# Ring loads of a weight stream pause around the reads of turned exponentials

## The chip, the cores and the metric

The kernel runs on one core of a Trainium2 chip. The metric is the device time of one execution in microseconds (us): the median of three runs is 900.81 us (900.17 to 900.99). The core has TensorE (PE, with its weight loads shown as PEld), VectorE (DVE), ScalarE (ACT), GpSimd (POOL) and SyncE (SP); SP issues nearly all DMAs of this kernel on one queue.

## The reference

The inputs are q, k and v of 8 batches, 8 heads, 576 tokens and 64 features, and the weights of a gated feed-forward layer (512 to 1536 to 512).

```python
scores = scale * np.matmul(q_c, k_c.transpose(0, 1, 2, 4, 3))   # chunks of 64 tokens
scores = scores - np.max(scores, axis=-1, keepdims=True)
attn = np.exp(scores)
attn = attn / (np.sum(attn, axis=-1, keepdims=True) + 1e-09)
out = np.matmul(attn, v_c)
...
x = out of all heads, one row of 512 per token                  # 4608 rows
rms = np.sqrt(np.mean(x * x, axis=-1, keepdims=True) + 1e-06)
xn = x / rms * rms_g
g = xn @ w_gate
silu = g * (1.0 / (1.0 + np.exp(-g)))
val = xn @ w_val
return (silu * val @ w_out).astype(np.float32)
```

## The kernel before, in words

Tokens go through in tiles of 512. The first three tiles (`PLAIN`) are computed plainly, each float32 product as three products of rounded high and low parts. The other six are taken two at a time, in three blocks (`for b in range(NB)`, L1237), by a scheme that computes a 2x2 product of blocks with seven products (`P1` to `P7`) in place of eight. The text calls b = 0, 1 and 2 block one, two and three.

A block has two halves. The up half is six calls of `up_pair` (L832), each with seven products, so 42 steps, numbered 0 to 41 by `step.n`; a step is 12 matmuls of 128x512. The down half has 42 more. At the end of each step, `step()` runs what the table `at` holds for that number. There the attention of the next block's tokens is put, four units of 256 tokens each. Unit n starts at step `PAIR_AT[n]` (2, 12, 22, 32), and its parts come at the offsets in `PAIR_STEPS`: scores at 0, `second` at 3, `third` at 5, `fourth` at 8. `second` turns the exponentials on VectorE and writes them to DRAM (`turn`, L359, two DMAs `away_e<-e`, L367). `third` reads them back in another layout (`turn_back`, L369, eight DMAs of 64 KB, `eT<-away_e`, L376). `fourth` multiplies them by the values on TensorE (`ps_o`, L393). So the reads of units 0, 1 and 2 stand in the program at the end of steps 7, 17 and 27, and the products that need them behind steps 10, 20 and 30. Block three carries no attention.

The weights of the up half's products lie in DRAM as 21 pieces of 1 MB. `ring_load` (L809) takes one of the 18 buffers of the pool `wts` and issues one DMA (L812, `wr<-wsd`). Piece m holds products 2m and 2m + 1, which from pair 1 on are steps 2m and 2m + 1. The first three pieces are loaded before the block. In the loop, `ring_load_ahead(n // 2)` keeps three pieces ahead, so that from step 6 on an even step s stands in the program with the load of piece s/2 + 2: piece 5 at step 6, piece 6 at step 8, 10 at step 16, 11 at 18, 15 at 26, 16 at 28. The same pool holds the products' inputs (`xp`) and results (`g`, `tt`), and the down half's weights (`wo`).

What sets the order: TensorE's instructions are kept in the order of the program (`manual_schedule`, L1155). In the down half ACT, DVE and SP are too (`IN_ORDER`, L1265). In the up half the framework's scheduler orders these: by priority, which is the place in the program unless `high_priority` moves it, among the instructions that its own timing takes to be ready and that have a buffer. Once ordered, SP's queue runs in that order, and an instruction that waits holds up those behind it.

Of the kernel before, what the change touches and what calls it, by code (L numbers as in the profile page):

```python
# [42 lines left out]
PAIR_STEPS = -4, 0, 3, 5, 8, 8, 8, 11, 13  # L43
# [3 lines left out]
PAIR_AT = 2, 12, 22, 32  # L47
# [13 lines left out]
NB = (NT - PLAIN) // 2  # L61
# [19 lines left out]
def tile_chunk_attn_swiglu(  # L81
# [40 lines left out]
    last = Last()  # L122
    wp = last.open("wp", 3)

    def urgent():

        return tc.high_priority(offset=URGENT)

    def bank(pool, name):
        return pool.tile([P, 512], F32, tag=pool_tag[id(pool)], name=name)  # L130
# [614 lines left out]
    def big(shape, dtype, name):  # L745
        return wts.tile(shape, dtype, tag="wts", name=name)
# [62 lines left out]
    def ring_load(n):  # L809
        if n < len(wsd):  # L810
            t = ring[n] = big([P, 2, 2, 2, KH], F32R, "wr")
            nc.sync.dma_start(t.rearrange("p n a m c -> p n (a m c)").bitcast(F32), wsd[n])  # L812

    def product(n, m, p, ps, start, stop):
        w = ring[n // 2][:, n % 2]
        xp = xside[p]
        for kt in range(2):
            cols = slice(kt * P, (kt + 1) * P)
            for i, (a, b) in enumerate(((0, 0), (0, 1), (1, 0))):
                nc.tensor.matmul(  # L820
                    ps,
                    w[:, a, m, cols],
                    xp[:, b, kt],
                    start=start and kt == 0 and i == 0,
                    stop=stop and kt == 1 and i == 2,
                    skip_group_check=True,
                )
# [1 line left out]
    def hold(name):  # L829
        return xs.tile([P, TT], F32, tag="xs", name=name)  # L830

    def up_pair(i, step, wos, tt, sums, last=None):  # L832

        g = big([P, 2, 2, TT], F32, "g")
        ps = [{} for _ in range(2)]
        kept = [{} for _ in range(2)]

        def bank_of(m, name, pool):
            ps[m][name] = bank(pool, f"ps_{name}")

        for k, p in enumerate(ORD if i else FIRST):
            n = 7 * i + p
            ring_load_ahead(n // 2)
            if i == NPR - 1 and k in (4, 6):
                wos.append(out_load(k // 2 - 2))
            for m in range(2):
                if p == P1:
                    bank_of(m, "a", ps_h)
                elif p in (P6, P5, P4):
                    bank_of(m, {P6: "b", P5: "c", P4: "d"}[p], ps_acc)  # L850
                b = ps[m][{P1: "a", P2: "a", P6: "b", P7: "b", P5: "c", P3: "c", P4: "d"}[p]]
                product(n, m, p, b, p in (P1, P6, P5, P4), p in (P2, P7, P3, P4))
            if k == 6 and last is not None:
                with urgent():
                    last()
            with urgent():
                after(p, ps, kept, g)
            if k == 1 and sums:
                sums.pop()()
            step()  # L860
        if i % PER == 0:
            tt.append(big([P, PER, TT], F32, "tt"))
        t = tt[-1][:, i % PER]

        def sum_up():
            nc.vector.tensor_tensor(t, g[:, 0, 1], g[:, 0, 0], op=ALU.subtract)
            nc.vector.tensor_tensor(g[:, 0, 1], g[:, 1, 1], g[:, 0, 1], op=ALU.subtract)

        sums.append(sum_up)
        return g, t  # L870
# [47 lines left out]
    def ring_load_ahead(n):  # L918
        while loaded[0] < min(n + AHEAD_R, len(wsd)):
            ring_load(loaded[0])  # L920
            loaded[0] += 1
# [10 lines left out]
    def out_load(n):  # L932
        t = big([P, PER, 2, OH], F32R, "wo")
        part = t[:, : osd[n].shape[1]].rearrange("p n a c -> p n (a c)")
        nc.sync.dma_start(part.bitcast(F32), osd[n])
        return t

    def split_high(src, ready):
        gh = tmp.tile([P, TT], F32R, tag="tmp", name="gh")
        nc.scalar.copy(gh, src)  # L940
        ready.append([gh])

    def split_low(src, pair):
        gl = gp.tile([P, TT], F32R, name="gl")
        nc.vector.tensor_tensor(gl, src, pair[0].bitcast(F32), op=ALU.subtract)  # L945
        pair.append(gl)
# [102 lines left out]
    def unit_steps(u, x):  # L1049

        both = 2 * u, 2 * u + 1

        def first():
            sc = two_banks(ps_a, "ps_s")
            for i in both:
                scores(i, sc)
            turned_softmax(u, sc)

        def second():
            for i in both:  # L1060
                turned_sum(i)
                turn(i)

        def third():
            for i in both:
                turn_back(i)

        def fourth():
            turned_values(u)

        def fifth():
            for i in both:
                turned_norm(i)

        def sixth():
            for i in both:
                turned_scale(i)

        return [
            lambda: load_unit(u),  # L1080
            first,
            second,
            third,
            fourth,
            fifth,
            sixth,
            lambda: turn_x(u),
            lambda: turn_x_back(u, x),
        ]
# [147 lines left out]
    for b in range(NB):  # L1237
        t = PLAIN + 2 * b
        at = early
        early = {}  # L1240
        if b + 1 < NB:
            u = 2 * t + 4
            for n in range(4):
                for k, f in enumerate(unit_steps(u + n, (x, x2)[n // 2])):
                    after_it = LAST_STEPS if b == 0 and n == 3 else PAIR_STEPS
                    at.setdefault(max(PAIR_AT[n] + after_it[k], 0), []).append(f)
            one, two, late = x_sides(x, x2, st)
            for n, f in enumerate(one[:2]):
                at.setdefault(PAIR_AT[1] + PAIR_STEPS[-1] + 4 + n, []).append(f)
            for n, f in zip(X_AT, one[2:] + two[:1] + two[4:] + two[1:4]):  # L1250
                at.setdefault(7 * NPR + n, []).append(f)
            early = {n: list(todo) for n, todo in enumerate(late)}
        step = Steps(at)
        gts, wos, tt, sums, ready = [], [], [], [], []

        def first_splits():
            for g, _ in gts[:2]:
                split_high(g[:, 0, 0], ready)
            split_low(gts[0][0][:, 0, 0], ready[0])

        for i in range(NPR):
            last_part = first_splits if i == NPR - 1 else None
            gts.append(up_pair(i, step, wos, tt, sums, last_part))
        loaded[0] = 0
        with tc.manual_schedule(engines=IN_ORDER):  # L1265
            down_pair(t, gts, wos, step, b + 1 < NB, sums, ready)
# [53 lines left out]
```

## Time and profile before

| what | value |
|---|---|
| median of three runs | 900.81 us (900.17 to 900.99) |
| profiled execution | 901.91 us, its span 900.1 us |
| granted TensorE clock, mean | 0.990 |
| PE, DVE, ACT, POOL busy | 98%, 67%, 51%, 20% of the span |
| mean DMA rate | 258 GB/s |
| loads of ring pieces (L812) | 63 of 1024 KB, 7.0 us to landing at the median |
| reads of exponentials (L376) | 112 of 64 KB, 3.6 us to landing at the median |

The span runs from the first to the last instruction; the profiled execution's own time is 1.8 us more. A row of the timeline gives the start, the length, the engine, the line, and what is written from what; the rows of SP are the issues of DMAs, not the transfers. Block one's up half runs from 355.2 to 482.5 us, that of block two from 540.7 to 666.8.

### The profile page before, as it was taken

What the parts mean: (1) busy time and instruction counts of PE and PEld (TensorE: products, weight loads), DVE (VectorE), ACT (ScalarE), POOL (GpSimd) and SP (SyncE); (2) the same over time, 40 slices, a digit from 0 to 9 for tenths busy, and PEclk for the clock granted to TensorE, in tenths of its full rate; (3) what the DMA queues carried; (4) which work ended last, traced back from release to release, by engine and by line L of the source; (5) the groups of instructions that cost most, each with busy time, mean ns of one, the idle gap of its engine ahead of it and who ended that gap; (6) DMA issues with size and microseconds to landing.
All of it is one profiled execution on the core that took longest, in us unless ns stands there. A gap on an engine that the chain in (4) does not pass through costs nothing.

```text
span 900.1 us, 17442 instructions
## 1 busy us (share of the span) xinstructions
PE 879.5 (98%) x6828; PEld 721.1 (80%) x6828; DVE 607.0 (67%) x962; ACT 455.9 (51%) x775; POOL 181.7 (20%) x157
## 2 busy tenths in 40 slices
PE   4899999999999999999999999999999999999998
PEld 3688888888888888887887888888878888888886
DVE  6999865464568755985677997556669953334776
ACT  5997934343435564545455644336547522222452
POOL 0003040243200000233233002333330004323200
PEclk9799999999999999999999999999999999999999
DMA  9699999777977865688977887687667784445442
GB/s 355 269 342 328 324 327 359 246 244 244 305 240 242 249 210 163 263 304 276 300 264 263 298 316 278 247 301 225 242 243 277 285 354 169 155 154 201 183 164 95
DMA packets 85794, 231.84 MB, mean 258 GB/s; under 512 B 8912, under 2 KB 45264, under 8 KB 71504
## 3 DMA queue, kind: packets, MB, share of 16 engines
q1 hardware_dynamic: 84656, 230.20, 72.5%
q8 instruction: 54, 0.88, 0.4%
q10 hardware_dynamic: 1056, 0.52, 0.2%
q14 instruction: 28, 0.23, 0.1%
HBM read 167.25 MB, written 63.44 MB: 256 GB/s over the span
## 4 chain that ended last, share of the span: by engine, by line
PE 84%; ACT 6%; DVE 4%; DMA 4%; issue 1%; POOL 1%; SPq 0%; ACTq 0%; DVEq 0%; POOLq 0%
PE ps_a L820 10%; PE ps_c L820 10%; PE ps_b L820 10%; PE ps_g L592 9%; PE acc L627 9%; PE ps_v L592 9%; PE ps_c L1033 5%; PE ps_b L1033 5%; PE ps_a L1033 5%; PE ps_d L820 5%; PE ps_d L1033 3%; PE ps_o L393 2%; PE ps_s L266 2%; DMA raw<-w_up_dram 1%; ACT w L178 1%
## 5 line engine op out<-in xcount | busy, mean ns | idle before, releaser
L820 PE MATMUL ps_b<-xp,wr 128*128 128x512 f32 x432 | 104.6, 391 | 0.0
L820 PE MATMUL ps_c<-xp,wr 128*128 128x512 f32 x432 | 104.0, 390 | 0.0
L820 PE MATMUL ps_a<-xp,wr 128*128 128x512 f32 x432 | 103.8, 390 | 0.0
L592 PE MATMUL ps_g<-xh,parts 128*128 128x512 f32 x288 | 96.8, 397 | 0.6 <-ACT xh L517 0.6
L592 PE MATMUL ps_v<-xh,parts 128*128 128x512 f32 x288 | 95.2, 391 | 0.4 <-DVE sg L614 0.4
L820 PEld LDWEIGHTS ps_c<-xp,wr 128*128 128x128 f32 x432 | 80.9, 188 | 16.9
L820 PEld LDWEIGHTS ps_a<-xp,wr 128*128 128x128 f32 x432 | 80.8, 188 | 17.0
L820 PEld LDWEIGHTS ps_b<-xp,wr 128*128 128x128 f32 x432 | 80.6, 188 | 17.0
L627 PE MATMUL acc<-parts,gh 128*128 128x512 f32 x288 | 89.9, 393 | 0.0
L908 POOL TENSOR_TENSOR g<-u,u 128x512 f32<-128x512 f32 x18 | 23.2, 1289 | 252.6 <-DVE u L904 141.3
L592 PEld LDWEIGHTS ps_g<-xh,parts 128*128 128x128 f32 x288 | 54.7, 190 | 12.8 <-ACT xh L517 1.0
L592 PEld LDWEIGHTS ps_v<-xh,parts 128*128 128x128 f32 x288 | 54.4, 189 | 12.0 <-DVE sg L614 0.8
L940 ACT CAST gh<-g 128x512 fp32r<-128x512 f32 x72 | 43.5, 621 | 37.9 <-PE ps_b L1033 13.2
L627 PEld LDWEIGHTS acc<-parts,gh 128*128 128x128 f32 x288 | 53.2, 188 | 11.2
L945 DVE TENSOR_TENSOR gl<-g,gh 128x512 fp32r<-128x512 f32 x72 | 49.2, 692 | 16.2 <-PE ps_a L1033 5.7
L876 ACT ACTIVATE p<-p 128x512 f32<-128x512 f32 x36 | 22.7, 632 | 70.2 <-POOL p L898 60.0
L898 POOL TENSOR_TENSOR p<-p,p 128x512 f32<-128x512 f32 x36 | 46.9, 1313 | 53.6 <-DVE rs L354 35.7
L592 PE MATMUL ps_g<-xl,parts 128*128 128x512 f32 x144 | 56.7, 394 | 0.0
L592 PE MATMUL ps_v<-xl,parts 128*128 128x512 f32 x144 | 56.3, 391 | 0.0
L627 PE MATMUL acc<-parts,gl 128*128 128x512 f32 x144 | 56.2, 390 | 0.0
L885 DVE TENSOR_TENSOR u<-ps_b,p 128x512 f32<-128x512 f32 x36 | 24.7, 687 | 41.2 <-PE ps_b L820 37.6
L820 PE MATMUL ps_d<-xp,wr 128*128 128x512 f32 x216 | 52.3, 391 | 0.0
(150 smaller groups left out, 1706.4 us busy)
## 6 DMA issues: line engine op xcount, KB each, us to landing
wr<-wsd SPq DMA_DIRECT2D x63, 1024.0 KB, 7.0
wo<-osd SPq DMA_DIRECT2D x30, 1024.0 KB, 7.7
raw<-w_up_dram SPq DMA_DIRECT2D x12, 1024.0 KB, 10.4
vt<-v_dram SPq DMA_DIRECT2D x18, 512.0 KB, 7.0
wsd<-parts SPq DMA_DIRECT2D x18, 512.0 KB, 8.4
qt<-qT_dram SPq DMA_DIRECT2D x17, 512.0 KB, 5.8
kt<-kT_dram SPq DMA_DIRECT2D x17, 512.0 KB, 6.8
away_e<-e SPq DMA_DIRECT2D x28, 256.0 KB, 3.3
```

The lines of the kernel that those rows point to most:

```text
L266: nc.tensor.matmul(st["s"][j][c * CH : (c + 1) * CH, pr], st["q"][rows, pr, tok : tok + CH], st["k"][rows, pr, tok : tok + CH], start=True ...
L393: nc.tensor.matmul(st["o"][(2 * c + t) * Q : (2 * c + t + 1) * Q, h * D : (h + 1) * D], eT[c][rows, t, h], vt[rows, c, h], start=True, sto ...
L592: nc.tensor.matmul(ps, a[f][:, cols], b[dt], start=(dt == 0 and i == 0), stop=(dt == NDT - 1 and i == 2),)
L627: nc.tensor.matmul(acc[s], a[:, cols], b, start=(f == 0 and i == 0), stop=(f == NF - 1 and i == 2),)
L820: nc.tensor.matmul(ps, w[:, a, m, cols], xp[:, b, kt], start=start and kt == 0 and i == 0, stop=stop and kt == 1 and i == 2, skip_group_ch ...
L876: nc.scalar.activation(t, t if src is None else src, AF.Silu)
L885: nc.vector.tensor_tensor(kp["u2"], b["b"], kp["p1"], op=add)
L898: nc.gpsimd.tensor_tensor(kp["p5"], kp["p1"], kp["p5"], op=add)
L908: nc.gpsimd.tensor_tensor(g[:, 0, 1], kp["u2"], kept[0]["u2"], op=mult)
L940: nc.scalar.copy(gh, src)
L945: nc.vector.tensor_tensor(gl, src, pair[0].bitcast(F32), op=ALU.subtract)
L1033: nc.tensor.matmul(banks[m][name], w[:, (0, 1, 0)[k], m * P : (m + 1) * P], (gh, gh, gl)[k], start=opens and i == 0 and k == 0, stop=not ( ...
```

## The change

In blocks one and two, `up_pair` does not call `ring_load_ahead` in the steps 6, 7, 16, 17, 26 and 27. The next call, in steps 8, 18 and 28, loads what was left out together with its own piece: 5 and 6, 10 and 11, 15 and 16. Odd steps load nothing from step 5 on in either version. No instruction is added or removed.

```diff
-    def up_pair(i, step, wos, tt, sums, last=None):
+    def up_pair(i, step, pauses, wos, tt, sums, last=None):
...
             n = 7 * i + p
-            ring_load_ahead(n // 2)
+            if step.n not in pauses:
+                ring_load_ahead(n // 2)
...
         step = Steps(at)
+        reads = [n + PAIR_STEPS[3] for n in PAIR_AT[:-1]] if b + 1 < NB else []
+        pauses = {n - k for n in reads for k in range(2)}
...
-            gts.append(up_pair(i, step, wos, tt, sums, last_part))
+            gts.append(up_pair(i, step, pauses, wos, tt, sums, last_part))
```

## Rows read from the trace of the kernel before

**Rows 1.** The page: span, and busy time of each engine.

```profile
span 900.1 us, 17442 instructions
...
PE 879.5 (98%) x6828; PEld 721.1 (80%) x6828; DVE 607.0 (67%) x962; ACT 455.9 (51%) x775; POOL 181.7 (20%) x157
```

**Rows 2.** Waits of PE, 355 to 482.6: us in total, times, longest.

```profile
PE ps_o L393 <- DMA eT<-away_e: 0.7, 2, 0.4
```

**Rows 3.** Timeline of PE, block one: start, length, what.

```profile
386.49 1.48 PE L393 MATMUL ps_o<-vt,eT 64*32 64x64 f32 x128
...
413.84 2.88 PE L820 MATMUL ps_d<-xp,wr 128*128 128x512 f32 x12
416.73 0.27 PE L393 MATMUL ps_o<-vt,eT 64*32 64x64 f32 x2
...
418.09 1.42 PE L393 MATMUL ps_o<-vt,eT 64*32 64x64 f32 x122 [0.26 <-DMA eT<-away_e]
```

**Rows 4.** The chain that ended last, 400 to 425: start, length, what.

```profile
408.14 8.06 DMA wr<-wsd
...
416.22 1.74 DMA eT<-away_e
```

**Rows 5.** Timeline of SP, block one.

```profile
357.23 2.03 SPq L812 DMA_DIRECT2D wr<-wsd  x4
...
378.93 3.68 SPq L376 DMA_DIRECT2D eT<-away_e  x8
...
383.60 0.44 SPq L812 DMA_DIRECT2D wr<-wsd  x1
...
398.80 1.10 SPq L812 DMA_DIRECT2D wr<-wsd  x1
...
408.14 0.45 SPq L812 DMA_DIRECT2D wr<-wsd  x1
411.19 5.33 SPq L376 DMA_DIRECT2D eT<-away_e  x8
...
436.60 0.42 SPq L812 DMA_DIRECT2D wr<-wsd  x1
438.26 3.92 SPq L376 DMA_DIRECT2D eT<-away_e  x8
```

**Rows 6.** Timeline of SP, block two.

```profile
542.55 1.44 SPq L812 DMA_DIRECT2D wr<-wsd  x3
...
560.45 0.42 SPq L812 DMA_DIRECT2D wr<-wsd  x1
560.97 5.09 SPq L376 DMA_DIRECT2D eT<-away_e  x8
566.10 1.38 SPq L812 DMA_DIRECT2D wr<-wsd  x3
...
591.04 5.18 SPq L376 DMA_DIRECT2D eT<-away_e  x8
...
620.97 0.42 SPq L812 DMA_DIRECT2D wr<-wsd  x1
621.76 4.80 SPq L376 DMA_DIRECT2D eT<-away_e  x8
```

**Rows 7.** Timeline of PE: steps 10, 30 of block one, then 10, 20, 30 of two.

```profile
383.68 2.88 PE L820 MATMUL ps_a<-xp,wr 128*128 128x512 f32 x12
...
445.37 2.88 PE L820 MATMUL ps_b<-xp,wr 128*128 128x512 f32 x12
...
569.23 2.88 PE L820 MATMUL ps_a<-xp,wr 128*128 128x512 f32 x12
...
599.39 2.88 PE L820 MATMUL ps_d<-xp,wr 128*128 128x512 f32 x12
...
629.55 2.88 PE L820 MATMUL ps_b<-xp,wr 128*128 128x512 f32 x12
```

**Rows 8.** The ring loads' line, whole span: from issue to landing.

```profile
DMA to landing us min/median/max: 4.7/7.0/13.0
```

## The prediction

> **What bounds the kernel now.** I read the page first. TensorE is busy for 879.5 of 900.1 us, 98% of the span [rows 1], so the order of SP's queue matters only where a DMA makes TensorE wait. The waits of TensorE come next. The diff touches two stretches, the up halves of blocks one and two. In the first the view has one row, two waits for the reads of the exponentials, 0.7 us together [rows 2]; in the second (540 to 668) the same view has none, and no wait for a ring load in either. TensorE's timeline then gives the price of that one place. The product of unit 0 with its values is one burst of 1.48 us; that of unit 1 starts at 416.73 and ends at 418.09 + 1.42 = 419.51, that is 2.78 us [rows 3]. So 1.30 us are lost there, in the whole stretch that the diff touches. The chain of waits tells why: from 408.14 a ring load of 8.06 us, and only behind its landing the last read, 1.74 us from 416.22 [rows 4]. A load in front of the reads did make them late, once. This 1.30 us, 0.14% of the time, is all that better placed ring loads can win there.
>
> **Which load it is.** I count the loads in SP's order. Three pieces are there before the block. Four are issued at 357.23 (pieces 3 to 6), then four single ones from 383.60 to 398.80 (7 to 10), so the one at 408.14 is piece 11 [rows 5]. In the program piece 11 stands at step 18, already one step behind the reads of step 17; the scheduler has pulled it ahead of them. The diff does not move piece 11. It moves piece 10 to piece 11's side.
>
> **The change part by part.** No operation comes or goes: 63 loads before and after, the same two writes and eight reads in each unit. What moves is the place in the program of six loads, all on SP's queue: pieces 5, 10 and 15 in two blocks, past the eight reads of units 0, 1 and 2. No wait is added by hand and no other queue is passed. What counts is whether the order that SP really runs follows.
>
> Piece 5, from step 6 to 8: in block one it goes out at 357.23, in block two at 542.55 with pieces 4 and 6 [rows 5, 6], over 20 us ahead of its step. Piece 6 is in the same bursts, and it already stands at step 8, where piece 5 goes. So that place does not keep a load from being issued at the block's start. Cost 0.
>
> Piece 10, from step 16 to 18: it goes out at 398.80 in block one, within step 14, and among the three loads at 566.10 in block two, at step 8 [rows 5, 6]. The reads of unit 1 are issued at 411.19 and 591.04, and nothing else that could be ready asks for a buffer between the old place and the new. Cost 0, by the same argument.
>
> Piece 15, from step 26 to 28, is the doubtful one. It is issued at 436.60, with the reads 1.66 us behind it at 438.26, and in block two at 620.97, with the reads 0.79 us behind at 621.76 [rows 5, 6]. Here a load that the diff moves stands just in front of reads. If the scheduler found the load ready and the reads not yet (they need the written exponentials to land), the load keeps its place whatever its rank. That this happens is shown twice: piece 11 at 408.14 went ahead of the reads of step 17 from a place in step 18, and piece 7 at 560.45 in block two ahead of the reads of step 7 from a place in step 10 [rows 5, 6]. If both were ready at once, the new rank puts the reads first. The bounds: nothing, or the cost of rival one below, 1.9 to 7.8 us. I take nothing, as the nearest rows are the two loads that did overtake.
>
> The sum: 0 us. The 1.30 us of unit 1 stays, since piece 11 stays. The cover for the 0 on the loads is the lead that they have now: piece 15 has 445.37 - 436.60 = 8.8 us until step 30 and in block two 629.55 - 620.97 = 8.6 [rows 5 to 7], against 7.0 us from issue to landing at the median [rows 8]. It is thin: 1.7 us later than now, a median landing is late.
>
> The profiled execution took 901.91 us for a span of 900.1 [rows 1], 1.8 us around it; it lies 1.1 us over the median of 900.81, within what single runs differ by. I put the 0 on the median: 900.8 us.
>
> **A rule for and a rule against.** The row: the last read of unit 1 came 1.74 us behind the landing of the 1 MB load issued in front [rows 4]. The Trainium skill (DMA: Bandwidth & Descriptors, section Two DMAs through the same engine are not ordered) says that within one queue of a DMA engine descriptors start in order, so small reads behind a large load begin behind it; the trace agrees. By that rule every load taken from the front of reads helps them; it is the mechanism of rival three. Against the change, the same page (section Rules for kernel authors, the row on overlapping DMA with compute) says to issue a DMA early and to wait late; by it the moved loads would be exposed, and that is the mechanism of rivals one and two, whose times are worked out from rows alone.
>
> **Rival one: piece 15 really goes behind the reads.** The reads need 3.68 us of issues where no load stands in front of them, 378.93 in block one [rows 5]. In block one they would be out at 438.26 + 3.68 = 441.94; with the shortest landing, 4.7 us, the piece is there at 446.64, and step 30 wants it at 445.37: 1.27 us late. In block two 621.76 + 3.68 + 4.7 = 630.14 against 629.55: 0.59 late [rows 5 to 8]. Together 1.9 us, to 902.7. With today's ends of the reads (442.18 and 626.56) and the median of 7.0 it is 3.81 + 4.01 = 7.8 us, to 908.6. I take the lower end, since the reads in front are small and the queue behind them is short. TensorE is in program order, so all of a late step is lost. For it: the load and the reads are neighbours in the queue. Against it: the two loads that overtook reads.
>
> **Rival two: the queue follows the program (slower).** This is the one on the other side. All six loads come behind their reads, while each is wanted two steps on, some 5.4 to 6 us later; it decides as soon as a load is issued less than 4.7 to 7.0 us ahead of its step. From today's ends of the reads, plus 7.0, less the start of the step: block one 382.61 + 7.0 - 383.68 = 5.9, 416.52 + 7.0 - 413.84 = 9.7, and 3.8; block two 566.06 + 7.0 - 569.23 = 3.8, 596.22 + 7.0 - 599.39 = 3.8, and 4.0 [rows 3, 5 to 8]. The sum is 31 us; with 4.7 us each it is 31 - 6 x 2.3 = 17. So 918 to 932, and I say 925. For it: that is what the text of the program says. Against it: pieces 5, 6 and 10 are issued today steps ahead of their place, so the queue does not follow the program.
>
> **Rival three: the reads of unit 1 get free.** If the new ranks let piece 11 fall behind the reads of block one's unit 1 while piece 10 stays at 398.80, the 1.30 us goes: 899.5. For it: rows 4 show this very delay. Against it: piece 11 keeps its place in the program, and if piece 10 came at 408.14 in its stead, the reads would stand behind a 1 MB load as before.
>
> That the change does nothing is not a rival but the forecast: the order of the queue stays, or changes only where nobody waits.
>
> **How the numbers follow.** A measurement of this kernel can tell about 0.2%, 1.8 us, from no change. Forecast, order as before: 0.71, 900.8, with the spread of the runs 900.2 to 901.1. Rival one: 0.14, 902.7, half of it over 1.8 us slower. Rival two: 0.08, 925. Rival three: 0.07, 899.5, within 0.2% unless the new order frees more than the trace shows, for which I leave 0.03. Slower is 0.07 + 0.08 and 0.01 for a shuffled order on the other engines: 0.16. Faster 0.03. Same 0.81. The range goes from 899.4 (rival three) to 903.4 (rival one with some more); it leaves out rival two and the upper part of rival one.
>
> **What would show it.** In the changed kernel's timeline of SP, pieces 5 and 6 in the bursts at about 357 and 543, piece 10 near 399 and 566, and one load between the writes and the reads of unit 2, near 437 and 621, show the forecast right step by step; one load left between the writes and reads of block one's unit 1, with TensorE's 0.7 us of waits for `eT`, shows that the stall stayed. A wait of TensorE for `wr` at steps 10, 20 or 30, or step 30 starting late, shows rival one or two. Unit 1's burst of 1.5 us shows rival three. The prediction is wrong if the order of ready instructions hangs on rank more than I take it to, or if a few ranks shifted by the loads reorder VectorE's or ScalarE's work in front of TensorE.

## The result: 1.0% slower, and the profile after

The changed kernel takes 909.75 us at the median of six runs (907.27 to 913.06) against 900.55 for the kernel before (900.17 to 901.1): a ratio of 1.0102, 95% interval 1.0089 to 1.0116. The forecast was 900.8, within 899.4 to 903.4. It was wrong.

The waits of TensorE in the changed kernel, in the up halves of blocks one and two, answer to [rows 2]. Each stretch now has a wait for a ring load; the wait for the reads is gone.

```profile
PE ps_d L820 <- DMA wr<-wsd: 3.9, 1, 3.9
PE ps_o L393 <- issue: 0.4, 1, 0.4
...
PE ps_d L820 <- DMA wr<-wsd: 2.0, 1, 2.0
```

Both are at step 20, the first user of piece 10, and nowhere else. TensorE's timeline, steps 18 to 20 of block one with unit 1's values (as [rows 3]), then steps 19 and 20 of block two:

```profile
408.07 2.88 PE L820 MATMUL ps_c<-xp,wr 128*128 128x512 f32 x12
410.79 2.88 PE L820 MATMUL ps_b<-xp,wr 128*128 128x512 f32 x12
417.55 4.53 PE L820 MATMUL ps_d<-xp,wr 128*128 128x512 f32 x12 [3.88 <-DMA wr<-wsd]
422.01 1.31 PE L393 MATMUL ps_o<-vt,eT 64*32 64x64 f32 x109
423.70 0.41 PE L393 MATMUL ps_o<-vt,eT 64*32 64x64 f32 x19 [0.37 <-issue]
...
601.23 2.88 PE L820 MATMUL ps_b<-xp,wr 128*128 128x512 f32 x12
606.12 4.58 PE L820 MATMUL ps_d<-xp,wr 128*128 128x512 f32 x12 [2.00 <-DMA wr<-wsd]
```

Undisturbed steps follow each other at 2.72 us (408.07 and 410.79), so step 20 was due at 413.51 and at 603.95. It is 4.04 and 2.17 us late. Then it also runs slowly, 4.53 and 4.58 us in place of 2.88: 1.65 and 1.70 more. Unit 1's values in block one take 424.11 - 422.01 = 2.10 us in place of 2.78, 0.68 less. The sum is 4.04 + 1.65 - 0.68 + 2.17 + 1.70 = 8.9 us, and the span grew by 8.7 (900.1 to 908.8). In this execution the whole loss is there.

The slow part is the granted clock. These are stretches of the changed kernel (length, busy time of PE, PEld, DVE, ACT, POOL, then the granted clock, DMA share, GB/s): up to the wait, the wait and step 20 in both blocks, and in block one what lies behind it.

```profile
404.00:413.50 9.50, 9.50 (x43) 7.68 (x41) 6.82 (x15) 5.09 (x8) 1.28 (x1) 1.00 0.76 219
413.50:417.50 4.00, 0.17 (x1) 0.00 (x0) 1.52 (x3) 0.63 (x1) 2.92 (x3) 1.00 0.93 340
417.50:422.00 4.50, 4.45 (x12) 3.12 (x12) 1.38 (x2) 0.63 (x1) 0.85 (x1) 0.62 1.02 424
422.00:430.00 8.00, 7.63 (x171) 6.14 (x174) 2.13 (x4) 4.22 (x11) 2.37 (x3) 1.00 0.77 318
596.00:604.00 8.00, 8.00 (x36) 6.38 (x34) 3.19 (x5) 2.51 (x3) 1.28 (x1) 1.00 0.68 196
604.00:606.10 2.10, 0.11 (x1) 0.01 (x1) 1.47 (x3) 0.00 (x0) 1.15 (x1) 1.00 1.00 414
606.10:610.60 4.50, 4.49 (x12) 3.33 (x12) 1.29 (x2) 1.07 (x2) 2.62 (x3) 0.62 1.02 431
```

TensorE is idle, then runs for 4.5 us at a mean of 0.62, most of it at the lower of its two levels (1.2 GHz). The DMA engines are busiest in the same stretches (1.02); experiment six below tells the two apart.

Why piece 10 is late stands in SP's timeline of the changed kernel, block one, which answers to [rows 5]:

```profile
392.11 0.38 SPq L812 DMA_DIRECT2D wr<-wsd  x1
...
398.46 0.50 SPq L234 DMA_DIRECT2D qt<-qT_dram  x1
...
406.67 1.08 SPq L367 DMA_DIRECT2D away_e<-e  x2
407.81 0.45 SPq L235 DMA_DIRECT2D kt<-kT_dram  x1
408.77 3.71 SPq L376 DMA_DIRECT2D eT<-away_e  x8
412.52 0.90 SPq L812 DMA_DIRECT2D wr<-wsd  x2
```

Piece 9 goes out at 392.11, then no ring load for 20 us; pieces 10 and 11 follow the reads at 412.52. Where piece 10 stood (398.80) there is now a load of queries. In the chain piece 10 takes 4.90 us from 412.52, and step 20 waits for its landing at 417.42:

```profile
412.52 4.90 DMA wr<-wsd
417.42 0.14 issue
417.55 4.53 PE ps_d L820 x12
```

In block two (as [rows 6]) two loads, not three, follow the reads of unit 0, and the other one heads the burst behind unit 1's:

```profile
570.27 0.90 SPq L812 DMA_DIRECT2D wr<-wsd  x2
...
595.61 5.36 SPq L376 DMA_DIRECT2D eT<-away_e  x8
601.00 2.59 SPq L812 DMA_DIRECT2D wr<-wsd  x5
```

Piece 5 is issued in the same burst as before in both blocks. Piece 15 goes out ahead of its reads, between the two writes, at 437.94 and 625.39, and no step 30 waits.

### The profile page after: what moved, and what is told of

The parts are those of the page before. It is cut to its first block, busy times and chain, and to the rows that moved or that the text cites. A ratio compares the mean times of both kernels' runs of the same rounds, so it can differ in the third digit from the quotient of the medians.

```text
span 908.8 us, 17440 instructions
## 1 busy us (share of the span) xinstructions
PE 882.4 (97%) x6828; PEld 722.9 (80%) x6828; DVE 608.9 (67%) x962; ACT 456.7 (50%) x775; POOL 184.3 (20%) x157
## 4 chain that ended last, share of the span: by engine, by line
PE 89%; DMA 5%; DVE 3%; ACT 1%; issue 1%; POOL 0%; SPq 0%; ACTq 0%; DVEq 0%
PE ps_g L592 11%; PE acc L627 11%; PE ps_v L592 11%; PE ps_a L820 10%; PE ps_c L820 9%; PE ps_b L820 9%; PE ps_c L1034 5%; PE ps_b L1034 5%; PE ps_a L1034 5%; PE ps_d L820 5%; PE ps_d L1034 3%; PE ps_o L393 2%; PE ps_s L266 2%; DMA raw<-w_up_dram 1%; DMA wr<-wsd 1%; DMA wo<-osd 1%
## 5 line engine op out<-in xcount | busy, mean ns | idle before, releaser
L820 PE MATMUL ps_d<-xp,wr 128*128 128x512 f32 x216 | 55.6, 409 | 5.9 <-DMA wr<-wsd 5.9
L820 PEld LDWEIGHTS ps_d<-xp,wr 128*128 128x128 f32 x216 | 42.3, 197 | 15.8 <-issue 4.3
```

Source lines behind the costliest of these rows:

```text
L820: nc.tensor.matmul(ps, w[:, a, m, cols], xp[:, b, kt], start=start and kt == 0 and i == 0, stop=stop and kt == 1 and i == 2, skip_group_ch ...
```

## The experiments

The theory after the result: when the framework orders the instructions, it gives out the buffers of the pool `wts` in the order in which the program first writes them. A load may then be pulled ahead of anything but the first write of an earlier tile of that pool. The result tile `g` of pair 2 is first written in step 17 (`after`, L892 in the changed kernel). Piece 10 in step 16 stood ahead of that write; in step 18 it stands behind it. One rival says that the place behind the reads of step 17 is what counts; another that a buffer was short.

**One unit at a time.** Experiment one keeps the pause only in steps 16 and 17, experiment two only in the others.

```diff
-        pauses = {n - k for n in reads for k in range(2)}
+        pauses = {n - k for n in reads for k in range(2)} & {16, 17}
...
+        pauses = {n - k for n in reads for k in range(2)} - {16, 17}
```

> Only piece 10 moves (the pause is kept in steps 16 and 17 alone), in both blocks. If piece 10's lateness is the whole loss, the time is that of the changed kernel, 908 to 911 us, with TensorE waiting for a ring load at step 20 of both blocks (3.9 and 2.0 us there). If every moved piece costs its share, it lies clearly between, 903 to 906.

> The counterpart: only pieces 5 and 15 move (the pause is kept in steps 6, 7, 26 and 27). If piece 10 alone is to blame, 900.6 us give or take 0.6, and no wait of TensorE for a ring load. If piece 15 behind or between the writes and reads of unit 2 costs something (the recorded rival one), 902.5 or more.

Experiment one measured 909.79 us, ratio 1.0095 (1.0078 to 1.0112) to the kernel before; experiment two 900.31, ratio 0.9991 (0.9982 to 1.0). Piece 10 alone makes the loss, pieces 5 and 15 cost nothing that the runs can tell. In the profile of experiment one step 20 is 5.66 us late in block one and 2.38 in block two, more than in the changed kernel. In block one it then takes 4.57 us. In block two it takes 2.98, at a granted clock of 1.00:

```profile
607.09 2.98 PE L820 MATMUL ps_d<-xp,wr 128*128 128x512 f32 x12 [2.21 <-DMA wr<-wsd]
```

So a late piece 10 makes step 20 late in both blocks, but the slow clock behind the wait does not always come.

**The first write of `g` moved ahead.** Experiment three leaves the change whole and gives `g` an early first writer.

```diff
         g = big([P, 2, 2, TT], F32, "g")
+        if i == 2 and pauses:
+            nc.gpsimd.memset(g[:, 0, 0, :1], 0.0)
```

> The change in full, and one tiny write (GpSimd sets one column of the pair's result tile g to zero at step 14 of blocks one and two; the column is written over in step 17), so that g has its first writer ahead of piece 10 in the program also in time. Theory: buffers of the pool are given out in the program's order, and piece 10 came late because its new place is behind the first write of g in step 17; then piece 10 goes out early again (near 399 and 570 us), and the time is 900.6 give or take 0.8. Rival: the rank behind the reads of step 17 is what held piece 10; its place in the program is still step 18, so it stays late and the time is 908 to 911.

It measured 900.46 us, ratio 0.9991 (0.998 to 1.0002). The loss is gone, though piece 10 still stands at step 18, behind the reads, in the program. SP's timeline of experiment three shows piece 10 back at 398.23 in block one. In block two three loads stand behind unit 0's reads again and a fourth, piece 11, follows at 579.77:

```profile
398.23 1.03 SPq L812 DMA_DIRECT2D wr<-wsd  x1
...
564.65 1.39 SPq L812 DMA_DIRECT2D wr<-wsd  x3
...
579.77 0.38 SPq L812 DMA_DIRECT2D wr<-wsd  x1
...
589.32 5.33 SPq L376 DMA_DIRECT2D eT<-away_e  x8
```

Piece 11 is a step-18 load in the kernel before too, and there it went out only behind unit 1's reads of block two. With `g` written early it goes out some 9.5 us ahead of those reads, where it had gone out 5.2 us behind the first of them (596.26 against 591.04 in the kernel before). This rules out the rank behind the reads as the cause.

**A buffer more.** Experiment four leaves the change whole and frees one buffer of the pool: it leaves out the input tile of product `P4` and its split and multiplies that of `P2` in its place, so what it computes is not the layer's output.

```diff
         def high(p):
+            if p == P4:
+                xside[p] = xside[P2]
+                return
             xside[p] = big([P, 2, 2, TT], F32R, "xp")
...
         def low(p):
+            if p == P4:
+                return
```

> The change in full, and one buffer of the pool freed for the whole up half: product P4 takes the input tile of P2 and its own split is left out, so the result of P4 is not the reference's. Theory of the program's order: a free buffer does not help, 908 to 911 us with the wait at step 20. Rival, shortage: piece 10 waited because no buffer was free; with one more it goes out early and the time is 900 to 902.

It measured 911.39 us, ratio 1.0104 (1.007 to 1.0138), with the ring loads again behind the reads of unit 1 (SP's timeline of experiment four):

```profile
407.20 4.77 SPq L376 DMA_DIRECT2D eT<-away_e  x8
412.36 0.81 SPq L817 DMA_DIRECT2D wr<-wsd  x2
```

One more free buffer changes nothing. It speaks against shortage; more than one was not tried. Experiment three speaks against it too: there `g` holds its buffer early (its first write is at 379.0), and piece 10 still finds one at 398.23.

**Either side of the write.** Experiments five and eight move piece 10 alone into step 17, five behind `after`, which writes `g`, eight ahead of the step's products.

```diff
+        pauses = {n - k for n in reads for k in range(2)} & {16, 17}
...
                 after(p, ps, kept, g)
+            if step.n == 17 and step.n in pauses:
+                ring_load_ahead(n // 2)
...
(the eighth:)
+        pauses = {n - 1 for n in reads} & {16}
```

> Piece 10 alone is moved, into step 17, behind the first write of g and ahead of the reads. Theory of the program's order: it still loses its early place (399 and 566 us), since g's first write stands ahead of it, but comes a little earlier than in the changed kernel: near 408 us in block one, among the reads of unit 1 near 592 in block two. Block one: landing near 408.3 + 6 to 8 = 414.3 to 416.3 against step 20 at 413.5, so 1 to 3 us late, plus 1.7 of slow clock; block two: 592 + 5 to 7 = 597 to 599 against 599.4, in time. So 903 to 906 us. Rival (the rank behind the reads is what counts): the load is ahead of the reads in the program, so it keeps its early place and the time is 900.6.

> Piece 10 alone is moved, by one step only, from step 16 to the start of step 17: ahead of the first write of g in that step, where the kernel of the fifth experiment had it behind that write. Theory of the program's order: it keeps its early places (399 and 566 us) and the time is 900.6 to 901.1, that of the kernel before. If any later place costs in proportion to the shift, 903 or more.

Experiment five measured 905.56 us, ratio 1.0064 (1.004 to 1.0087); experiment eight 900.61, ratio 1.0003 (0.9993 to 1.0012). Both places are in step 17 and ahead of the reads. SP's timeline of experiment five, block one:

```profile
408.78 1.08 SPq L367 DMA_DIRECT2D away_e<-e  x2
...
410.41 0.45 SPq L812 DMA_DIRECT2D wr<-wsd  x1
410.95 6.12 SPq L376 DMA_DIRECT2D eT<-away_e  x8
```

and of experiment eight:

```profile
398.36 1.06 SPq L812 DMA_DIRECT2D wr<-wsd  x1
```

Behind the write the load goes out 12 us later than ahead of it (410.41 and 398.36), although the reads still come behind it. On the chip it does not wait for the write. VectorE's timeline of experiment five has the write of `g` at 411.00, 0.59 us behind the load:

```profile
411.00 0.69 DVE L894 TENSOR_TENSOR g<-ps_a,c 128x512 f32<-128x512 f32 x1 [0.31 <-ACT c L879]
```

So the order comes from the framework, fixed before the kernel runs. The ten runs of experiment five spread from 902.55 to 911.51, and the profile stands for one at 904.62. In it step 20 waits in block one alone, where unit 1's values also wait 0.21 us for the reads behind the load:

```profile
416.89 3.00 PE L820 MATMUL ps_d<-xp,wr 128*128 128x512 f32 x12 [1.10 <-DMA wr<-wsd]
...
420.34 1.43 PE L393 MATMUL ps_o<-vt,eT 64*32 64x64 f32 x122 [0.21 <-DMA eT<-away_e]
```

**TensorE kept busy while it waits.** Experiments six and ten are the changed kernel with matmuls in front of step 20; nine is the changed kernel again, on the chip of ten.

```diff
+FILL = 18, 10
...
+                if step.n == 20 and m == 0 and pauses:
+                    xp = xside[P2]
+                    for _ in range(FILL[len(fills)]):
+                        nc.tensor.matmul(
+                            b, xp[:, 0, 0, :P], xp[:, 0, 0], start=True, stop=True, skip_group_check=True
+                        )
+                    fills.append(1)
                 product(n, m, p, b, p in (P1, P6, P5, P4), p in (P2, P7, P3, P4))
...
+    fills = []
```

> The change in full, with TensorE kept busy while it waits at step 20: 18 matmuls (block one) and 10 (block two) on an input tile, whose results the step's own first matmul overwrites, stand ahead of the step's products. In the changed kernel step 20 takes 4.53 and 4.58 us in place of 2.88, at a granted clock of 0.61, after 3.9 and 2.0 us of idleness. Theory: the slow stretch comes from the idleness; then step 20 takes 2.88, and the time is 909.6 less 2 x 1.7, that is 906.3 give or take 1. Rival: the slow stretch has another cause (traffic, the load itself); then it stays and the time is 909.6 or more.

> The changed kernel once more, beside the next one on the same chip: 909 to 910 us, step 20 taking 4.5 to 4.6 us in both blocks behind its wait.

> The changed kernel with TensorE kept busy in front of step 20 once more, beside the unfilled one. In the first look the slow stretch was gone (2.88 and 3.02 us for step 20), but the median was 909.3 where 906.3 was expected. If the slow stretch is worth its 3.3 us, it lies 2 to 3.3 under the unfilled kernel on the same chip; if the filling costs as much as it gives, within 1.

Six measured 909.34 us (908.12 to 909.95), nine 909.71 (908.95 to 910.56), ten 908.75 (907.78 to 909.34). Six was expected at 906.3 and missed that. Between nine and ten the filling gains about 1.0 us, not the 2 to 3.3 expected; with four runs of each, that gain is hardly clear of the noise (an estimate of its 95% interval from these eight runs goes from -0.1 to 2.2). The traces show that without the idleness the slow clock does not come, and why the sum was too large. TensorE's timeline of experiment six, step 20 of both blocks behind the filling:

```profile
413.72 4.24 PE L857 MATMUL ps_d<-xp 128*128 128x512 f32 x18
418.61 3.02 PE L821 MATMUL ps_d<-xp,wr 128*128 128x512 f32 x12 [0.65 <-DMA wr<-wsd]
...
602.98 2.43 PE L857 MATMUL ps_d<-xp 128*128 128x512 f32 x10
605.25 2.88 PE L821 MATMUL ps_d<-xp,wr 128*128 128x512 f32 x12
```

Step 20 with DMA as busy as in the changed kernel (1.01), but at the full clock; experiment six, block two, in the form of the stretches above:

```profile
603.00:607.00 4.00, 4.00 (x19) 3.34 (x18) 1.50 (x3) 0.63 (x1) 2.94 (x3) 1.00 1.01 426
```

TensorE's timeline of the changed kernel in experiment nine, and SP's of its block two:

```profile
418.60 4.57 PE L820 MATMUL ps_d<-xp,wr 128*128 128x512 f32 x12 [4.30 <-DMA wr<-wsd]
...
606.67 2.97 PE L820 MATMUL ps_d<-xp,wr 128*128 128x512 f32 x12 [1.38 <-DVE p L898]
...
601.69 2.58 SPq L812 DMA_DIRECT2D wr<-wsd  x5
```

With the filling no step 20 is slow, at the same traffic, so the load and the traffic are not what slows it. But the slow stretch is not paid each time without it: in experiment nine block two ran step 20 in 2.97 (the row names VectorE; piece 10, issued at 601.69, landed 4.8 us later, at 606.5, just ahead of the step; in the kernel before, step 20 of block two starts at 599.39, ahead of that operation of VectorE at 599.62, and so does not need it). Of the four profiles with piece 10 behind the reads and no filling (the changed kernel, experiments one, four and nine), block one's step 20 is slow in all (4.30 to 4.57 us), block two's in the changed kernel alone (4.58; 2.98, 3.00 and 2.97 in the others). And a filling of 2.27 us, from 602.98 to 605.25, costs more than a wait of some 1.5. The clock's share of the loss is thus 3.35 us in one of these four executions and 1.4 to 1.7, from block one alone, in the other three; most of the rest is lateness.

**Piece 11 behind the reads.** Experiment seven adds one edge to the kernel before, in block one: the load of step 18 is issued behind the last read of unit 1.

```diff
-                nc.sync.dma_start(eT[c][dst].rearrange("p t h q -> p t (h q)"), back[c, k])
+                state["read"] = nc.sync.dma_start(
...
-            ring_load_ahead(n // 2)
+            if step.n in hold_at:
+                with tc.issue_after(state["read"].ins):
+                    ring_load_ahead(n // 2)
...
+            gts.append(up_pair(i, step, {18} if b == 0 else (), wos, tt, sums, last_part))
```

> The kernel before, with one edge in the order: in block one, piece 11 is issued behind the reads of unit 1 (the recorded rival three made real); piece 10 keeps its early place. Piece 11 would go out near 413 and land near 420, ahead of step 22 at 421. Theory: the reads are in time, the 1.3 us in front of unit 1's values go, and the time is 0.0 to 1.4 us under the kernel before, 899.5 at the best (in two of the runs so far the order of before had no such stall, so the mean gain may be less than 1.3). Rival: piece 11 is late itself, 902 or more.

It measured 900.91 us, ratio 1.0 (0.9991 to 1.0009). The order came out as meant, and unit 1's values ran without a wait:

```profile
409.58 4.68 SPq L376 DMA_DIRECT2D eT<-away_e  x8
414.31 0.42 SPq L814 DMA_DIRECT2D wr<-wsd  x1
```

```profile
416.42 1.48 PE L395 MATMUL ps_o<-vt,eT 64*32 64x64 f32 x128
```

Yet no time was won. The delay of [rows 3] is not paid in each execution. In the profile of experiment two, with piece 11 still in front of the reads (SP's timeline, then TensorE's), unit 1's burst took 1.49 us:

```profile
407.85 0.45 SPq L812 DMA_DIRECT2D wr<-wsd  x1
409.72 5.10 SPq L376 DMA_DIRECT2D eT<-away_e  x8
...
416.36 1.49 PE L393 MATMUL ps_o<-vt,eT 64*32 64x64 f32 x128
```

Experiments three and eight have the same order there, with bursts of 1.73 and 1.48 us. So 1.30 us was the price in one execution, and no version here beats the kernel before by more than 0.1%.

## Why the prediction was wrong, point by point

- **The bound was right.** TensorE was at 98%, and all that the change did to the time is a wait of TensorE for a DMA at one step of each block, with the slow clock behind some of these waits.
- **Piece 5: right,** cost 0, same bursts. **Piece 15: right in sum.** It stayed ahead of the reads in both blocks, and experiment two puts both pieces at no cost.
- **Piece 10 is the step that failed:** "nothing else that could be ready asks for a buffer between the old place and the new. Cost 0, by the same argument." I counted only instructions that could be ready. What lies between the two places is the first write of `g` in step 17, not ready by far, and the framework still places it first. Experiments three, five and eight show it: moving that write ahead of the load, or the load ahead of that write, restores the time, and the place against the reads does not decide. The term put at 0 measured 4.04 and 2.17 us of lateness, with 1.65 and 1.70 of slow clock.
- **The argument from piece 6 was the trap.** Piece 6 is pulled ahead from step 8, so step 8 looked a safe place. But pair 1's `g` is first written in step 10, and `tt`, of the same pool, at the end of step 8, both behind either place of piece 5. That pair 2's is in step 17 was in the code, and the rows of before show the borders: three loads at 566.10 [rows 6], pieces 8 to 10 of steps 12 to 16, all between the writes of `g` in steps 10 and 17; the next four, 11 to 14, of steps 18 to 24, went out together behind unit 1's reads, between the writes of steps 17 and 24. For pieces 7 to 14 of block two the bursts are cut where the writes are; later ones are not (17 and 18, on either side of the write in step 31, go out together at 627.61). In SP's timeline of the kernel before:

```profile
596.26 2.25 SPq L812 DMA_DIRECT2D wr<-wsd  x4
```

- **Rival two named the price, for the wrong reason.** It had piece 10 behind the reads, 9.7 us late in block one and 3.8 in block two by the median landing, 7.4 and 1.5 by the shortest. It was 4.04 and 2.17. Block two lies between its ends. Block one was over-sized, since I took the end of the reads of before (416.52) with piece 11 in front; with that load behind, they end at 412.48. Its sum for all six loads does not apply: the queue did not follow the program, one load did.
- **The clock was missing from every rival.** I priced a late load by its lateness alone; 1.65 and 1.70 us of slow clock came with it in the profiled execution, about half of that in three others.
- **Rival three** came true by half in the changed kernel: piece 11 fell behind the reads and 0.68 of the 1.30 us went, but piece 10 fell behind them too, at a loss thirteen times as large. Alone, in experiment seven, it was worth nothing measurable.
- **The spread was read too narrow.** The profiled execution lay 1.1 us over the median, "within what single runs differ by"; the three runs then on record go only from 900.17 to 900.99. Later runs of the kernel before, from 899.02 to 902.91, bear the sentence out.

## What to carry to other kernels

Where a framework hands out the buffers of a shared pool as this one does, a load that is moved in the program can be pulled ahead only as far as the first write of the tile before it. List the first writers of every tile of the pool between the old place and the new one, ready or not. Read the bursts of loads in the queue before the change: where they are cut can show those borders, though not each of them did here. And when a load may lose its lead, price the loss as the lateness and, for TensorE, what a slow clock may add behind the wait (here nothing to 1.7 us a step).

## What the hardware showed that was not expected

- The length of TensorE's wait alone did not tell whether the slow clock followed. In block two a step 20 that came 2.17 us late ran for 4.5 us at a granted clock of 0.62 (the changed kernel), and one that came 2.38 us late ran at 1.00, in 2.98 (experiment one). Steps that came about 1.3 and 1.5 us late (experiments five and nine) ran in 3.00 and 2.97. What makes the difference is open.
- The same order in SP's queue made unit 1's reads 1.30 us late in one execution and not at all in another (bursts of 2.78 us in the kernel before and 1.49 in experiment two). One profiled execution prices such a delay badly.
